# Retention and a low-rank mixer on one core: every engine's order planned by a list scheduler inside the kernel, persistent buffers, and the first u^T built in PSUM from x

## The chip, the cores and the metric

The kernel runs on one core of a Trainium2 chip. A core has a matrix engine (TensorE, "PE" in the profile; "PEld" is its loading of weights), VectorE (DVE), ScalarE (ACT), GpSimd (POOL) and SyncE (SP), which here only issues DMA transfers. In these traces each engine works through its own instructions in the order that the program gives to it, so an instruction that waits holds up all behind it. PE's results go to PSUM, which both kernels divide into eight banks of 128 x 512 float32, and the other engines copy them from there to SBUF.

The metric is device time in microseconds (us), lower is better. The kernel before takes 380.89 us (median of three runs, 378.45 to 381.08).

## The reference, cut to what matters

```python
# batch 8, heads 8, seq 576, head_dim 64  ->  d_model 512, d_ff 2048, rank 32
scores = scale * q @ k^T
ret    = scores * Dmat[h]          # Dmat = gamma_h^(i-j) for i >= j, else 0
x      = (ret @ v)                 # laid out as (batch, seq, heads*head_dim)
u      = x + V^T @ (U^T @ x)       # mixes along the sequence, rank 32
out    = u + relu(u @ w_ch1) @ w_ch2
```

Both kernels factor the decay into a scale on v and one on the result, keep a running state k^T v per chunk of 128 rows, and work on bf16 tiles with float32 sums. Two batches are 1152 rows, which are nine chunks of 128. Chunk 4, called `XC`, holds the last 64 rows of one batch and the first 64 of the next. Counted in batches there are eight groups of work; each consists of a "front" (load q, k and v, transpose q and k, scores, retention, x, U^T x, u, transpose u) and an MLP (two large matrix products, Y1 with w_ch1 and Y2 with w_ch2). The even groups' MLPs have four chunks, the odd ones' five.

The MLPs are most of the work. While PE does the MLP of one group, the front of the next is slipped in between. So the kernel has a start without any MLP (the first front), a stretch in which the weights are still being loaded, and then a steady state.

## The kernel before

Every front is a list of items with an estimated cost, and so is every MLP. A small function merges the two lists by cost shares, and what it emits is the order of PE, POOL and SP. The order on VectorE and ScalarE is left to the framework.

```python
def interleave(main, fill, lead=0.0, end=1.0):
    tm = sum(c for c, _ in main) or 1
    tf = sum(c for c, _ in fill) or 1
    i = j = 0
    dm = df = 0.0
    while i < len(main) or j < len(fill):
        if j >= len(fill) or (
            i < len(main) and dm / tm <= lead + (end - lead) * df / tf
        ):
            dm += main[i][0]
            main[i][1]()
            i += 1
        else:
            df += fill[j][0]
            fill[j][1]()
            j += 1
# [...] the pools, the constants, the items themselves
        def T(c):                                    # transpose q and k of a chunk
            # [...]
            if not pe_transpose:
                nc.sync.dma_start_transpose(
                    out=qkT, in_=t[:, 0:2, :, :].rearrange("p j h d -> p (j h d)")
                )
                return
            # [...] eight transposes on PE, one copy on ACT
# [...]
    with tc.manual_schedule(engines={PE, POOL, SPQ}):
        early_consts()
        for c in A_CH:
            load_chunk(0, c)                         # k, q, v of a chunk, float32, on SP
            if c == 1:
                load_mixer()
            if c == 3:
                load_w1([0])                         # weights: DMAs that cast, on POOL's queue
        interleave([], front_items(0, [], True, 0))  # only this front transposes on PE
        load_w1(range(1, dff // W1B))
        load_w2()
        for a in chunks_of(1):
            load_chunk(*a)
        for g in range(2 * NP):
            main = mlp_items(g // 2, g % 2, sts[g // 2])
            fill = front_items(g + 1, chunks_of(g + 2)) if g + 1 < 2 * NP else []
            interleave(main, fill, 0.35 if g == 0 else 0.05, 0.9)
```

`lead` and `end` say over which part of the MLP's time the front is spread. Line numbers such as L426 in the profile are lines of this file: L214 the DMA transpose of q and k, L237 the running state, L254 the scores, L281 their mask on VectorE, L294 retention times v, L361 U^T x, L366 its copy by ACT (`a_sb`), L376 and L379 the way back (V), L390 the DMA transpose of u, L426 Y1 and L437 Y2.

## Time and profile before

| | before |
|---|---|
| median of three runs | 380.89 us |
| span of the profiled run | 381.3 us |
| PE busy | 329.2 us, 86% |
| DVE, ACT, POOL busy | 37%, 32%, 16% |
| first matmul of the first MLP | 41.8 us |
| first matmul of the second MLP; its u^T complete | 93.0; 95.6 us |
| last matmul ends | 377.3 us |

The page of the profile first. The first line gives busy time, share of the span and instructions of each engine. The rows `PE`, `PEclk` and `DMA` cut the span into 40 slices of 9.5 us and give the busy share, the granted TensorE clock and the DMA engines' busy share in tenths (9 is 90% or more). The last line shown gives shares of the chain that ended last, followed back from the last instruction.

```profile
...
PE 329.2 (86%) x2440; PEld 176.1 (46%) x2440; DVE 142.9 (37%) x199; ACT 123.2 (32%) x244; POOL 62.4 (16%) x86
...
PE   2655794887997999999998989998999999999995
...
PEclk9999996799899999999999999999999999999999
DMA  9999999995995149995994279997991480040012
...
PE 56%; DMA 18%; SPq 13%; DVE 6%; issue 3%; ACT 2%; POOL 1%; DVEq 0%; POOLq 0%
...
```

PE is full nearly everywhere from slice 11 on; the first ten slices are poor, and there the DMA engines are at 9. Only 56% of the chain is PE. Slices 7 and 8 also show a clock of 0.6 and 0.7. The same by stretch, from the windows view (us of the window, then busy time with the number of instructions of each engine, the clock, DMA share and GB/s; the DMA share counts overlapping packets and is not used here):

```profile
...
0.00:41.80 41.80, 20.61 (x194) 13.14 (x195) 20.32 (x41) 11.96 (x17) 22.62 (x44) 1.00 1.22 194
41.80:95.60 53.80, 42.08 (x255) 18.57 (x255) 17.53 (x23) 12.87 (x22) 14.63 (x16) 0.90 1.10 184
95.60:343.00 247.40, 232.23 (x1788) 124.49 (x1788) 101.62 (x130) 84.78 (x174) 25.16 (x27) 0.99 0.80 142
343.00:381.30 38.30, 34.27 (x204) 19.90 (x204) 3.46 (x5) 13.56 (x31) 0.00 (x0) 1.00 0.11 42
...
```

In the second window PE is busy for 42.08 of 53.80 us, in the third for 232.23 of 247.40: 11.7 and 15.2 us without any matmul. The fourth, the last MLP alone, has nothing in it that could be gained. (In the first stretch PE has little to do at all.) What PE waits for is in the view of waits (engine, tile and line, what ended the wait, us in total, number of times, the longest):

```profile
...
PE po L294 <- DVE ret L281: 9.6, 10, 2.6
...
PE psc L254 <- DMA qkT<-qkv: 5.7, 2, 4.6
...
PE ph L376 <- ACT a_sb L366: 2.7, 4, 0.7
PE ps_y_936 L426 <- DMA uT<-ut: 1.9, 1, 1.9
PE ps_y_2800 L426 <- DMA uT<-ut: 1.6, 1, 1.6
...
```

These are short waits: for the masked scores, for a DMA transpose of q and k, for `a_sb`, and for the transposes of u by DMA with which every MLP starts. The longest one after the start lies in the second stretch. PE's timeline (start, us, the matmuls, and in brackets the idle time before them with what ended it):

```profile
...
56.30 1.03 PE L426 MATMUL ps_y_622<-uT,w_sb 128*128 128x512 bf16 x4
61.98 0.60 PE L254 MATMUL psc<-qkT 64*128 64x128 bf16 x8 [4.65 <-DMA qkT<-qkv]
...
62.73 1.89 PE L426 MATMUL ps_y_648<-uT,w_sb 128*128 128x512 bf16 x4
...
```

PE stands still for 4.65 us and then runs the same four matmuls at 1.89 us that took 1.03 before. It waits for a transpose that the DMA queue of SP issued late; in SP's timeline two transposes hold the queue for 14 us:

```profile
...
46.74 14.01 SPq L214 DMA_TRANSPOSE qkT<-qkv  x2
...
```

### The profile page before, as it was taken

To read this page: it belongs to the slowest core of one execution; us is meant where nothing else is said; L and a number is where in the kernel's file an instruction comes from. 1 tells how busy PE (TensorE), PEld (TensorE's weight loads), DVE (VectorE), ACT (ScalarE), POOL (GpSimd) and SP (SyncE) were. 2 spreads that over 40 slices of the span, in tenths; PEclk is the share of its full clock that TensorE was granted. 3 is DMA by queue.
4 is the path that set the end of the run, shared out by engine and by line. 5 is a ranking of instruction groups with operands and counts; after the bars stand their busy time and mean duration, and the time that the engine had idled before them with its cause. 6 is when DMAs were issued, how large, how long until landed. Compare 5 with 4: busy or idle time off the path is not lost.

```text
span 381.3 us, 5987 instructions
## 1 busy us (share of the span) xinstructions
PE 329.2 (86%) x2440; PEld 176.1 (46%) x2440; DVE 142.9 (37%) x199; ACT 123.2 (32%) x244; POOL 62.4 (16%) x86
## 2 busy tenths in 40 slices
PE   2655794887997999999998989998999999999995
PEld 1432341433673444544664435444764445447642
DVE  4454201555252342544335324552544424340021
ACT  3322361200572006501771035303660056007600
POOL 2746821221022000121021001220121000000000
PEclk9999996799899999999999999999999999999999
DMA  9999999995995149995994279997991480040012
GB/s 181 206 210 179 199 196 186 206 185 132 191 212 97 57 110 194 202 211 136 175 228 83 73 126 218 186 173 157 218 196 40 114 153 2 28 125 29 0 57 83
DMA packets 173659, 54.81 MB, mean 144 GB/s; under 512 B 164864, under 2 KB 169024, under 8 KB 173632
## 3 DMA queue, kind: packets, MB, share of 16 engines
q1 hardware_dynamic: 167840, 50.09, 73.6%
q0 software_dynamic: 5792, 4.34, 7.5%
q8 instruction: 19, 0.31, 0.4%
q14 instruction: 8, 0.07, 0.1%
HBM read 37.00 MB, written 9.44 MB: 122 GB/s over the span
## 4 chain that ended last, share of the span: by engine, by line
PE 56%; DMA 18%; SPq 13%; DVE 6%; issue 3%; ACT 2%; POOL 1%; DVEq 0%; POOLq 0%
DMA stage_t<-in_q_dram 8%; SPq L190 7%; DMA uT<-ut 4%; SPq L214 4%; DMA stage_t<-in_v_dram 3%; DVE ret L281 3%; PE po L294 2%; PE psc L254 2%; PE psa L361 2%; PE ph L379 1%; SPq L390 1%; DVE o_sb L443 1%; DVE qkv L194 1%; DMA qkT<-qkv 1%; DMA U_A<-in_moe_U_dram 1%
## 5 line engine op out<-in xcount | busy, mean ns | idle before, releaser
L426 PEld LDWEIGHTS <-w_sb 128*128 128x128 bf16 x768 | 72.2, 100 | 55.9 <-issue 17.3
L195 POOL TENSOR_TENSOR qkv<-stage_t,vscale 128x512 bf16<-128x512 f32 x36 | 38.1, 1060 | 216.2 <-DMA stage_t<-in_v_dram 156.0
L281 DVE TENSOR_TENSOR ret<-psc,tri 128x1024 bf16<-128x1024 f32 x32 | 39.1, 1223 | 50.9 <-PE psc L254 50.9
L194 DVE CAST qkv<-stage_t 128x1024 bf16<-128x1024 f32 x36 | 25.8, 718 | 64.4 <-DMA stage_t<-in_q_dram 64.4
L300 DVE TENSOR_TENSOR xt<-po,qscale 128x512 bf16<-128x512 f32 x36 | 24.8, 689 | 17.6 <-PE po L294 17.5
L366 ACT ACTIVATE a_sb<-psa 128x512 bf16<-128x512 f32 x8 | 4.8, 597 | 80.5 <-PE psa L361 76.5
L385 DVE TENSOR_TENSOR ut<-ph,xt 128x512 bf16<-128x512 f32 x36 | 24.6, 689 | 14.5 <-PE ph L379 14.4
L294 PE MATMUL po<-qkv,ret 128*128 128x64 bf16 x288 | 15.6, 201 | 9.6 <-DVE ret L281 9.6
L254 PE MATMUL psc<-qkT 64*128 64x128 bf16 x288 | 16.0, 238 | 8.8 <-DMA qkT<-qkv 5.7
L294 PEld LDWEIGHTS <-ret 128*128 128x128 bf16 x288 | 13.5, 103 | 19.6 <-DVE ret L281 15.1
L244 ACT ACTIVATE s_sb<-pss 128x512 bf16<-128x512 f32 x32 | 19.0, 593 | 5.4 <-PE pss L237 5.4
L254 PEld LDWEIGHTS <-qkT 64*128 64x128 bf16 x288 | 9.1, 102 | 22.3 <-issue 10.1
L237 PEld LDWEIGHTS <-qkv 128*128 128x128 bf16 x128 | 10.5, 105 | 6.9 <-issue 1.9
L237 PE MATMUL pss<-qkv 128*128 128x128 bf16 x112 | 12.0, 235 | 1.8 <-ACT s_sb L244 1.0
L437 PEld LDWEIGHTS <-y_3686 128*128 128x128 bf16 x80 | 7.8, 98 | 9.3
L437 PEld LDWEIGHTS <-y_929 128*128 128x128 bf16 x80 | 7.8, 101 | 9.3 <-issue 1.1
L437 PEld LDWEIGHTS <-y_1861 128*128 128x128 bf16 x80 | 7.6, 98 | 8.6
L437 PEld LDWEIGHTS <-y_2793 128*128 128x128 bf16 x80 | 7.6, 98 | 8.6
L221 PE MATMUL pst<-ident,qkv 128*128 128x128 bf16 x40 | 5.2, 311 | 7.3 <-DVE qkv L194 7.3
L226 ACT ACTIVATE qkT<-pst 128x1024 bf16<-128x1024 bf16 x5 | 5.1, 1024 | 15.1 <-PE pst L221 15.1
L163 POOL DMA_DIRECT2D w_sb<-in_moe_w_ch_dram x16 | 9.3, 597 | 3.5 <-DMA w_sb<-in_moe_w_ch_dram 3.5
L437 PEld LDWEIGHTS <-y_1457 128*128 128x128 bf16 x64 | 6.1, 98 | 7.1
(522 smaller groups left out, 536.7 us busy)
## 6 DMA issues: line engine op xcount, KB each, us to landing
out_dram<-o_sb SPq DMA_DIRECT2D x36, 256.0 KB, 2.2
stage_t<-in_k_dram SPq DMA_DIRECT2D x32, 256.0 KB, 3.9
stage_t<-in_q_dram SPq DMA_DIRECT2D x32, 256.0 KB, 5.1
stage_t<-in_v_dram SPq DMA_DIRECT2D x32, 256.0 KB, 5.1
w_sb<-in_moe_w_ch_dram POOLq DMA_DIRECT2D x16, 128.0 KB, 7.2
w_sb<-in_moe_w_ch_dram POOLq DMA_DIRECT2D x8, 256.0 KB, 11.5
stage_t<-in_k_dram SPq DMA_DIRECT2D x8, 128.0 KB, 4.8
stage_t<-in_q_dram SPq DMA_DIRECT2D x8, 128.0 KB, 4.8
```

The costliest lines, as they stand in the source:

```text
L190: nc.sync.dma_start(out=f[rows, j, :, :], in_=dram[b, :, t0:t0 + L, :].rearrange("h s d -> s h d"),)
L194: nc.vector.tensor_copy(out=t[:, 0:2, :, :], in_=f[:, 0:2, :, :])
L195: nc.gpsimd.tensor_tensor(out=t[:, 2, :, :], in0=f[:, 2, :, :], in1=vscale[:, c, :, None].to_broadcast([P, H, D]), op=ALU.mult,)
L237: nc.tensor.matmul(pss[:, hp, :], t[:, 1, 2 * hp:2 * hp + 2, :].rearrange("p h d -> p (h d)"), vt[:, 2 * hp:2 * hp + 2, :].rearrange("p h ...
L244: nc.scalar.activation(out=s_sb, in_=pss, func=AF.Copy)
L254: nc.tensor.matmul(psc[:, hl, hp, :], qkT[pb:pb + HALF, NHP + hp, :], qkT[pb:pb + HALF, hp, :], start=True, stop=True,)
L281: nc.vector.tensor_tensor(out=ret.rearrange("p (hp hl) i -> p hl hp i", hl=2), in0=psc, in1=mask[:, None, None, :].to_broadcast([P, 2, NHP ...
L294: nc.tensor.matmul(po[:, hl, hp * D:(hp + 1) * D], ret[:, h, :], t[:, 2, h, :], start=(c == 0 and hp == 0), stop=True, skip_group_check=True,)
L300: nc.vector.tensor_tensor(out=xt.rearrange("p (hp hl d) -> p hl hp d", hl=2, d=D), in0=po[:, :, 0:NHP * D].rearrange("p hl (hp d) -> p hl ...
L385: nc.vector.tensor_tensor(out=ut, in0=ph, in1=st["x", c], op=ALU.add)
L426: nc.tensor.matmul(ps[:, 0:n], w1_sb[:, cc, f * P:(f + 1) * P], uT[:, cc, t0:t0 + n], start=(cc == 0), stop=(cc == NCC - 1),)
L437: nc.tensor.matmul(ps, st["y1"][:, f, i * P:(i + 1) * P], w2_sb[:, f, :], start=(f == 0), stop=(f == NF - 1),)
```

## The change

The merging function goes. The kernel now describes each piece of work as an `Op` with a duration on its engine, dependencies, a priority and the buffers that it takes and gives back, and simulates all five engines and the DMA rings at build time. Of the operations that could start earliest, the one with the best priority is emitted next. The outcome fixes the order of all engines. Four further changes come with it: the buffers are persistent slots; the second group's fronts transpose on PE (no DMA transposes while the weights load); the first u^T is built directly in PSUM, as x^T (16 PE transposes) plus four matmuls that add V^T (U^T x), with U padded by zeros to 128 columns; and the weights come by plain float32 DMAs on SP and are cast by POOL or VectorE. Y1 of the odd groups goes from two halves of 320 columns to 512 + 128, and the stores go from SP to POOL's queue. The diff, cut to its core:

```diff
-def interleave(main, fill, lead=0.0, end=1.0):
-    [...]
+class Plan:
+    LAT = {"PE": 230.0, "ACT": 80.0, "DVE": 80.0, "POOL": 90.0}
+    DMA_LAT = 1700.0
+    DMA_AHEAD = 4500.0
+    [...]
+    def run(self):
+        [...]
+        def add(o):
+            o.ready = max([d.vis for d in o.deps], default=0.0)
+            for e, dur in o.engs:
+                avail[e].append((o, dur))
+        [...]
+                t, o, dur = min((c for c in cand if c[0] <= te + 1e-6), key=lambda c: c[1].prio)
+                k = (te, o.prio)
+                if best is None or k < best[0]:
+                    best = (k, e, o, dur, te)
+            [...]
+            if e == "SP":
+                ring = max(ring, t + 700.0) + o.work
+                o.vis = ring + self.DMA_LAT
 [...]
+    def load(p, c, which="AB", prio=0.0, first=True, early=False):
+        [...]
+        for o, (j, dram) in enumerate(((1, k), (0, q), (2, v))):
+            [...]
+            got[j] = DMA(470.0 * L / P + 60 * (n - 1), 1180.0 * L / P, fn, prio=prio + 0.01 * o,
+                         acq=[("stage", key)] if o == 0 else (), deps=[got[1]] if o else ())
 [...]
+    def ST(p, c, prio, half=None):                 # running state, in the bank ps_s
+        [...]
+        o = pl.op("PE", 230.0 + (190 if half else 0), fn,
+                  [st["v", c, w], st["k", c, w], None if first else prev], prio,
+                  acq=[("pss", ("S", p, c if first else 0))] if first else ())
 [...]
+        def xT(c, cc):                             # first u^T: x^T into PSUM ...
+            def fn(e):
+                mm(acc(cc)[:, c * P:(c + 1) * P], xs[slot("x", (0, c))][:, cc * P:(cc + 1) * P],
+                   ident, start=(c == 0), stop=True)
+            return fn
+        [...]                                      # ... plus (U^T x)^T V on top of it
+                mm(acc(cc), a_sb[0][:, cc * P:(cc + 1) * P], VV[:, 0:4 * P], start=False, stop=True)
 [...]
+    start_batch()
+    load_w(-800.0)
+    [...]
+    mlp(0, fixed(10.0, 10.0 + W, NU(0)))
+    front(1, dict(at=lambda n: -100.0 + n, load=500.0, cast=1, tr=2), pe=True)
+    for g in range(1, NG):
+        [...]
+            lo, hi = (0.02, 0.88)
+        [...]
-    with tc.manual_schedule(engines={PE, POOL, SPQ}):
-        [...]
+    with tc.manual_schedule():
+        for o, e in pl.run():
+            o.fn(e)
```

In `load`, q and v depend on `got[1]`, the DMA of k, and in the planner an operation becomes ready at its dependencies' `vis`, which for a DMA is its landing. And in `ST`, the first chunk of a running state takes the PSUM bank `pss` whenever it is free; the U^T x of the group before takes the same bank.

## The prediction

> **What bounds the kernel now.** PE is busy 86% of 381 us (the page). Counting all matmul columns at full rate (2.4 per ns: four 512-column matmuls per 0.86 us), PE needs 302.5 us, so 78 us are lost. PE's timeline shows three stretches:
>
> 1. 0 to 41.8 us (first MLP matmul, L426): about 10 us of PE work. Five q/k/v chunks are loaded; then the first u^T is built serially: psa at 32.4, four rounds of ph, DVE add, PE transpose, ACT copy, 1.8 us each.
> 2. 41.8 to 95.6 us (second group's MLP): about 40 us of work in 54. L426 takes 1.71 us per four until 46.8 and again from 62 to 70, where the slices show clock 0.6 and 0.7. The Trainium skill ("TensorE: Matmul & The Clock Gate", Part 1) says that a sparsely used array runs at half rate; this trace agrees (1.71 against 0.86 us). PE stands 4.65 us for a DMA transpose; the DMA queue's timeline shows two transposes holding SP for 14 us.
> 3. 95.6 to 381: 286 us for about 258 us of columns. From 95 to 343 the matmuls' starts exceed their columns' time by 22.8 us: some 4 are a fixed 2.5 ns each, 3 a halved clock, 10 the switches around 64-row matmuls, the rest waits for uT, a_sb and scores. The last group (343 to 377) loses nothing; 3.5 us of add and store follow.
>
> **What the change does.** Columns rise to 306.3 us (more transposes on PE). HBM bytes stay 37 MB. Weights move from casting DMAs on POOL's queue to plain DMAs on SP with 16 casts on POOL and DVE (a DVE cast of 128x1024 took 0.72 us; on POOL I estimate 1.2 to 2). The casting packets had 25.8 us of 16 engines; I estimate the same for plain ones, so the DMA floor for two groups and the weights stays at 60 us. The gain is order. In the instruction order, w1 blocks stand before the first group's last q, so its MLP hardly starts earlier: 36 to 41 us. But the second group uses no DMA transposes, and the first u^T needs only U^T x, four matmuls and four evictions.
>
> **Sum (estimates).** Stretch 1: -3. Stretch 2: second MLP at 83 instead of 95.6, a further -9. Stretch 3: uT, a_sb and score waits hidden by the order, -8; less halved clock, -3. Slips of a fixed plan against real DMA times, and POOL issuing 34 stores between scalings of v: +3. Total -20, and up to -6 more if the plan holds well: **355 us, 8 times in 10 between 342 and 369**. Chances: faster by over 2% 0.93, within 2% 0.05, slower 0.02.
>
> **What would show it.** Right: first MLP matmul near 38 us, second group's near 83; no PE wait over 2 us after 50; no clock of 0.6 in the slices; excess over columns from there to the last group under 15 us; no 14 us of transposes on SP. Wrong: PE waiting for POOL (late casts, w2 above all), DMA share well below 1 in the first 60 us because SP is blocked on buffers, or new waits for transposes where a planned DMA comes late.
>
> **What would make it wrong.** With fixed orders on all engines, one late DMA stalls all behind it; POOL casts may be much slower than planned. Conversely, if plain weight loads beat the casting ones, stretch 2 shrinks more and the time nears 342.

## The result

| | before | after |
|---|---|---|
| median of four runs | 380.72 us | 356.68 us |
| lowest to highest | 378.45 to 381.08 | 354.47 to 358.27 |
| ratio, 95% interval | | 0.9366 (0.9317 to 0.9415) |

The ratio is the mean time of one kernel's runs over that of the other's of the same rounds, so it is not quite the ratio of the medians. The result is right. Executions over 1.5% slower than the fastest of the same kernel are left out of the means. The kernel is 24.0 us faster by the medians. The profiled run of the changed kernel happens to be its fastest, so the spans of the two profiles (381.3 and 352.6) differ by 28.7 us, a little more than the kernels do; what follows splits those 28.7.

The page of the profile after, the same lines:

```profile
...
PE 319.7 (91%) x2520; PEld 167.2 (47%) x2520; DVE 156.1 (44%) x215; ACT 128.2 (36%) x214; POOL 63.7 (18%) x88
...
PE   0464699999999979998999999999999999999994
...
PEclk9995999999999999999999999999999999999998
DMA  8999999999999999999999948954213300150012
...
PE 80%; DMA 12%; SPq 3%; DVE 2%; issue 1%; ACT 1%; POOL 0%; DVEq 0%; ACTq 0%
...
```

PE's busy share rises to 91%, from the sixth slice on it is full, and 80% of the chain that ended last is PE. The clock of 0.6 in slices 7 and 8 is gone, but a 5 stands in the fourth slice. By stretch, cut at the same events as before:

```profile
...
0.00:44.20 44.20, 19.47 (x227) 13.56 (x227) 22.51 (x45) 17.28 (x27) 10.63 (x22) 0.88 1.05 222
44.20:82.10 37.90, 37.47 (x304) 18.92 (x298) 23.59 (x34) 17.38 (x29) 9.85 (x10) 1.00 1.05 260
82.10:310.00 227.90, 224.97 (x1779) 115.83 (x1777) 104.73 (x131) 81.61 (x139) 40.55 (x52) 1.00 0.76 156
310.00:352.60 42.60, 37.80 (x223) 18.91 (x221) 5.27 (x8) 11.94 (x20) 2.70 (x5) 0.97 0.17 53
...
```

In the second window PE now lacks 0.4 us, and in the third 2.9 of 227.9. Counted from event to event (starts of the first and second MLP, last matmul, end):

| stretch | before | after | difference |
|---|---|---|---|
| 1: start to first MLP | 41.8 | 44.2 | +2.4 |
| 2: first to second MLP | 51.3 | 37.9 | -13.4 |
| 3: second MLP to last matmul | 284.3 | 265.7 | -18.6 |
| tail | 3.9 | 4.8 | +0.9 |

So stretch 1, for which a part of the change was written, became longer, and the gain comes from the other two.

Not all of it is waiting. PE also works at half clock, and the clock row hides most of that: the trace's clock record begins with the first change, and what comes before counts as full. PE's timeline of the kernel before shows what the clock was. Groups of four matmuls of Y1 start 1.71 us apart in the opening (43.41, 45.12, 46.83), where the row says 9, and 0.86 to 0.87 apart after the first record, at 47.1 (47.82, 48.69, 49.55):

```profile
...
43.41 1.91 PE L426 MATMUL ps_y_532<-uT,w_sb 128*128 128x512 bf16 x4
...
47.82 1.03 PE L426 MATMUL ps_y_550<-uT,w_sb 128*128 128x512 bf16 x4
...
```

In all 14 traces the matmuls of a burst are spaced at half rate up to the first record (but for the first pair of a burst, which is closer). The record stands at 22.3 us after and between 20.4 and 60.5 in the other runs. From the traces follows an estimate of what this is worth. For every matmul that starts at half clock, take its columns at the half-rate spacing of this trace less those at the full-rate spacing: the sum is 19.5 us before (9.5, 6.7 and 3.3 in the three stretches) and 6.1 after (all in the first). PE's idle time up to the last matmul falls from 48.1 to 28.1 us. So of the 28.7 us, 20.0 are idle time and 13.4 are half clock; 3.8 of more matmul columns and 0.9 of tail go the other way. In stretch 2 alone 9.5 are idle time and 6.7 half clock. This is bookkeeping, not an experiment: PE idles and runs at half clock in the same places, and a faster clock in front of a late load may only have made PE wait longer there.

The waits of PE after, as above:

```profile
...
PE ps_big_t L334 <- DVE qkv_t L280: 12.5, 3, 5.6
...
PE ps_s L237 <- DVE qkv_t L287: 3.8, 4, 1.9
PE ps_big_t L237 <- DMA uT_t<-u_t: 2.0, 2, 1.8
PE ps_o L237 <- DVE ret_t L418: 1.9, 2, 1.6
...
```

All waits of the first two lines lie before 45 us, but for one of 0.3 at 50.5. After that, the longest is 1.8 us, once, for a transpose of u. The start of the kernel shows where stretch 1 went. PE's timeline:

```profile
...
30.64 0.61 PE L334 MATMUL ps_big_t<-ident,qkv_t 128*128 128x128 bf16 x4 [5.63 <-DVE qkv_t L280]
...
40.60 0.38 PE L237 MATMUL ps_s<-qkv_t 64*128 64x128 bf16 x4 [1.95 <-DVE qkv_t L287]
...
44.24 1.04 PE L237 MATMUL ps_big_t<-uT_t,w_sb 128*128 128x512 bf16 x4
...
```

PE stands 5.63 us until VectorE has cast a q. The chain that ended last names the DMA that was late, issued at 20.93 and landed 9.21 us later:

```profile
...
20.93 9.21 DMA stage_t<-in_q_dram
...
```

It is the last q of the first group. On SP's queue it stands behind three 512 KB weight blocks issued at 16.94 and two k of the second group, because the planner lets q wait for the landing of its k and uses the gap for the weights. Then, at 40.60, PE waits 1.95 us for the v of a second-group chunk, with the four matmuls that complete the first u^T standing behind it in PE's order. The first MLP could have started without either.

### The profile page after: what moved, and what is told of

Its sections match the earlier page's. It is cut to its first block, busy times and chain, and to the rows that moved or that the text cites. A ratio compares the mean times of both kernels' runs of the same rounds, so it can differ in the third digit from the quotient of the medians.

```text
span 352.6 us, 6119 instructions
## 1 busy us (share of the span) xinstructions
PE 319.7 (91%) x2520; PEld 167.2 (47%) x2520; DVE 156.1 (44%) x215; ACT 128.2 (36%) x214; POOL 63.7 (18%) x88
## 4 chain that ended last, share of the span: by engine, by line
PE 80%; DMA 12%; SPq 3%; DVE 2%; issue 1%; ACT 1%; POOL 0%; DVEq 0%; ACTq 0%
PE ps_big_t L237 67%; PE ps_s L237 5%; DMA stage_t<-in_q_dram 4%; PE ps_o L237 4%; DMA stage_t<-in_v_dram 4%; PE ps_sc L237 3%; DMA wst_t<-in_moe_w_ch_dram 2%; DMA uT_t<-u_t 2%; SPq L266 1%; DVE o_sb L666 1%; PE ps_big_t L334 1%; SPq L787 0%; DVE qkv_t L287 0%; DVE ret_t L418 0%; ACT s_sb L375 0%
## 5 line engine op out<-in xcount | busy, mean ns | idle before, releaser
L237 PE MATMUL ps_big_t<-uT_t,w_sb 128*128 128x512 bf16 (+1 forms) x768 | 134.5, 326 | 2.0 <-DMA uT_t<-u_t 2.0
L237 PE MATMUL ps_big_t<-w_sb,y_t 128*128 128x512 bf16 x576 | 133.9, 379 | 0.0
L618 ACT ACTIVATE y_t<-ps_big_t 128x512 bf16<-128x512 f32 x128 | 76.1, 597 | 63.0 <-PE ps_big_t L237 63.0
L237 PEld LDWEIGHTS <-y_t 128*128 128x128 bf16 x576 | 54.9, 98 | 63.5
L666 DVE TENSOR_TENSOR o_sb<-ps_big_t,u_t 128x512 f32<-128x512 f32 x36 | 24.9, 690 | 69.6 <-PE ps_big_t L237 69.3
L287 POOL TENSOR_TENSOR qkv_t<-stage_t,vscale 128x512 bf16<-128x512 f32 x30 | 31.5, 1051 | 98.3 <-DMA stage_t<-in_v_dram 56.1
L481 DVE TENSOR_TENSOR x_t<-ps_o,qscale 128x512 bf16<-128x512 f32 (+1 forms) x37 | 25.5, 690 | 51.1 <-PE ps_o L237 51.1
L418 DVE TENSOR_TENSOR ret_t<-ps_sc,tri 128x1024 bf16<-128x1024 f32 (+1 forms) x34 | 40.4, 1189 | 14.3 <-PE ps_sc L237 14.3
L672 POOL DMA_DIRECT2D out_dram<-o_sb x34 | 19.6, 576 | 138.8 <-DVE o_sb L666 134.8
L280 DVE CAST qkv_t<-stage_t 128x1024 bf16<-128x1024 f32 (+2 forms) x37 | 27.7, 749 | 25.1 <-DMA stage_t<-in_q_dram 24.7
L334 PE MATMUL ps_big_t<-ident,qkv_t 128*128 128x128 bf16 (+1 forms) x80 | 7.9, 250 | 17.4 <-DVE qkv_t L280 12.5
L237 PEld LDWEIGHTS <-qkT_t 64*128 64x128 bf16 (+1 forms) x552 | 14.7, 99 | 11.3 <-issue 6.8
L558 DVE TENSOR_TENSOR u_t<-ps_s,x_t 128x512 bf16<-128x512 f32 x20 | 13.7, 687 | 12.6 <-PE ps_s L237 12.5
```

The source lines that it names most:

```text
L237: nc.tensor.matmul(*a, skip_group_check=True, **kw)
L280: nc.vector.tensor_copy(**args)
L287: eng.tensor_tensor(out=t[rows, 2, :, :], in0=f[rows, 2, :, :], in1=vscale[rows, c, :, None].to_broadcast([L, H, D]), op=ALU.mult,)
L334: nc.tensor.transpose(pst[:, j * NHP + hp, rows], t[rows, j, 2 * hp:2 * hp + 2, :].rearrange("p h d -> p (h d)"), ident[rows, rows],)
L418: nc.vector.tensor_tensor(out=ret[slot(*rk)].rearrange("p (hp hl) i -> p hl hp i", hl=2)[rows, :, :, rows], in0=ps_sc[rows, :, :, rows], i ...
L481: nc.vector.tensor_tensor(out=xs[slot(*xk)].rearrange("p (hp hl d) -> p hl hp d", hl=2, d=D)[rows], in0=ps_o[rows, :, 0:NHP * D].rearrange ...
```

## The experiments

Twelve kernels ran, each beside the kernel before on the same chip. "Stretches" are those of the table above, from the profiled run. All results agree with the reference. One run of b_end80 (390.73) and two of a_wcast were slow; the medians include them, the ratios do not. Medians of different batches of runs differ by a microsecond or two for the kernel before (380.12, 382.31, 380.38 and 379.68), so the ratios are the better measure.

| kernel | median | ratio to before (95%) | stretches 1 / 2 / 3 | half clock: opening + recorded |
|---|---|---|---|---|
| before | 380.72 | 1 | 41.8 / 51.3 / 284.3 | 47.1 + 17.1 us |
| after | 356.68 | 0.937 (0.932 to 0.942) | 44.2 / 37.9 / 265.7 | 22.3 + 10.2 us |
| a_earlyq | 415.94 | 1.092 (1.083 to 1.100) | 36.8 / 64.2 / 306.7 | 21.0 + 78.5 us |
| a_noxt | 370.67 | 0.973 (0.967 to 0.979) | 67.7 / 33.4 / 263.7 | 22.7 + 44.4 us |
| a_dmat | 367.53 | 0.966 (0.959 to 0.974) | 46.8 / 47.9 / 266.6 | 22.0 + 27.3 us |
| a_auto | 357.67 | 0.939 (0.933 to 0.945) | 46.6 / 38.6 / 268.0 | 46.8 + 3.4 us |
| b_pe1 | 380.81 | 0.996 (0.992 to 1.000) | 42.2 / 52.4 / 280.2 | 44.7 + 6.8 us |
| b_end80 | 386.33 | 1.007 (1.000 to 1.014) | 42.2 / 48.8 / 286.0 | 47.0 + 13.7 us |
| b_manual | 417.73 | 1.093 (1.087 to 1.098) | 52.1 / 55.1 / 303.6 | 57.4 + 30.7 us |
| a_wcast | 357.99 | 0.929 (0.923 to 0.935) | 49.9 / 41.3 / 263.5 (slow run) | 44.4 us |
| a_earlyq_ps | 364.17 | 0.953 (0.947 to 0.960) | 37.9 / 55.7 / 265.6 | 20.4 + 20.5 us |
| a_y320sp | 362.28 | 0.950 (0.944 to 0.956) | 47.2 / 38.1 / 270.6 | 47.0 + 6.8 us |
| best1 | 348.70 | 0.915 (0.910 to 0.920) | see below | 28.3 us |
| best1_noxt | 356.48 | 0.938 (0.933 to 0.943) | 55.8 / 35.0 / 261.1 | 60.5 us |

The half-clock column gives first the opening, from the start to the first clock record, which the spacing of the matmuls shows to be at half rate, and then the sum of the later stretches in which the record shows 0.5 and that start before the last matmul.

### a_earlyq: let q and v of the first group be issued behind k's issue, not behind its landing

```diff
 [...]  # `soft`, a new field of Op, empty by default
         def add(o):
-            o.ready = max([d.vis for d in o.deps], default=0.0)
+            o.ready = max([d.end if d in o.soft else d.vis for d in o.deps], default=0.0)
 [...]
+            if early and p == 0 and c <= XC and which != "B" and o:
+                got[j].soft = (got[1],)
```

> The changed kernel, but the q and v loads of the first group are issued right behind k instead of after k has landed in the plan. In the changed kernel's trace PE waits 5.63 us for the last q of the first group (issued at 20.93, landed 30.14 behind three weight blocks) and reaches the first MLP matmul at 44.2 us. Theory (after that matmul PE never lacks work, so each us of an earlier start is a us of time): first MLP matmul at 35 to 39 us, no half clock at 25 to 35, time 5 to 8 us lower. Rival (the DMA floor of about 60 us for two groups and the weights binds): the start is earlier but PE waits later, between 45 and 80 us, for weights or second-group chunks, and the time moves by less than 2 us.

Measured: 415.94 us, slower than before by 9%. Both theories fell, though the first half of one held: the first MLP starts at 36.8, 7.4 us earlier. Everything after that is worse. One changed readiness gave a different plan for the whole kernel. PE's timeline of this run:

```profile
...
69.66 0.38 PE L238 MATMUL ps_s<-qkv_t 128*128 128x128 bf16 x4 [2.47 <-POOL qkv_t L290]
71.92 0.38 PE L238 MATMUL ps_s<-qkv_t 128*128 128x128 bf16 x4 [1.88 <-POOL qkv_t L290]
...
90.79 2.29 PE L238 MATMUL ps_s<-x_t,UU 128*128 128x512 bf16 x5 [0.74 <-ACT s_sb L378]
...
```

At 69.66 and 71.92 PE waits for POOL's scaling of a v. These matmuls are the running state of the third group, and they have taken the bank `ps_s` before the second group's U^T x, which needs the same bank. That U^T x comes only at 90.79, and the second MLP starts at 101.0. The lag is handed on from group to group: a front that comes late is then done in one piece with no MLP work in between, PE waits for each short step (in this run's view of waits 16.1 us in 16 waits for masked scores), and the sparse use shows in the clock, which falls to half again and again:

```profile
...
PEclk9986999866999969995699988997799977999999
...
```

The simulation inside the kernel says so too: the planned end that the kernel's own code computes at build time is 397 us for this kernel and 342 for the changed one. It is no measured time and lies 19 and 15 us below the medians, but it ranks them rightly.

### a_earlyq_ps: the same, and the running state may take the bank only after the previous group's U^T x

One dependency is added to a_earlyq:

```diff
-                  [st["v", c, w], st["k", c, w], None if first else prev], prio,
+                  [st["v", c, w], st["k", c, w], (ld.get("MA") if p or half else None) if first else prev], prio,
 [...]
         o = MA(p, par, t(nn + 0.9), bank)
+        ld["MA"] = o
```

> a_earlyq (early q and v loads, 416 us) with one more dependency in the plan: the running state of group g may take the PSUM tile ps_s only after the U^T x of group g-1 has used it. Theory (a_earlyq lost its time because the third group's running state took ps_s at 70 us and the second group's U^T x, due at 78, stood until 91, and this lag was handed on from group to group): 358 to 368 us, PE idle after the second MLP's start back below 6 us instead of 24.9, the second MLP at 84 to 92. Rival (the time went because the PE array lacked work at the start and its clock fell; the order is not the cause): 400 us or more, half-clock stretches after 100 us as in a_earlyq.

Measured: 364.17 us. This theory held in its time (its second MLP, at 84 to 92, was missed by 1.6 us): 52 us come back by one dependency, so who takes the shared bank first is what made a_earlyq slow. Stretch 1 is 37.9 and stretch 3 as good as after's (265.6 against 265.7). Stretch 2 is still 17.8 us longer than after's: its second MLP starts at 93.6. The early start of the first MLP brought nothing in this plan: between the two MLPs PE waits 7.3 us for casts of w2 blocks that landed late (four waits on L818, the longest 3.4), and half clock is recorded for 10.2 us.

### a_noxt: the first u^T as in the other groups, through u and a transpose of u

```diff
-        banks = [("big", "ucc0"), ("big", "ucc1"), ("sc", "ucc"), None]
-        [...]  # x^T and V^T (U^T x) into PSUM, four copies to uT
-            MH(0, 0, c, 20.0 + c, c)
+            MH(0, 0, c, base + 61 + c, c)
+            MT(0, 0, c, base + 61 + c, pe=True, first=c == 0)
```

> The changed kernel with one part undone: the first u^T is built as before (ph, DVE add, four PE transposes and an ACT copy per chunk) instead of in PSUM. Theory (the part shortens the serial tail before the first MLP matmul): first MLP matmul 3 to 5 us later than 44.2, time 3 to 5 us higher. Rival (the second group's data bounds that stretch anyway): the time rises by less than 1 us, PE standing less between 45 and 80.

Measured: 370.67 us, 14 us slower than the changed kernel, with a first MLP at 67.7: neither the 3 to 5 us of the theory nor the less than 1 of its rival. Not all of this is the cost of the older path. The planner also put a transpose of a second-group chunk in front of the last pieces of the first u^T, and its q had not been cast:

```profile
...
59.65 0.61 PE L334 MATMUL ps_big_t<-ident,qkv_t 128*128 128x128 bf16 x4 [7.01 <-DVE qkv_t L280]
```

The clock had fallen to half long before this wait, at 26.1, and stayed there without a break for 44.4 us (fourth to eighth slice):

```profile
...
PEclk9995555699999999999999999999999999999999
...
```

The stretch 2 that follows is shorter than after's (33.4 against 37.9), since the second group's work has been done in the meantime. So this run shows that the part and the plan cannot be judged apart: it gives 14 us as the worth of the part under this plan. The run best1_noxt, below, gives another figure under a better one.

### a_dmat: the second group transposes by DMA again

```diff
-            if pe:
+            if pe and c == XC:
                 t_pe(p, c, w, t(n) - 1.0, first=w != "B")
 [...]
-            MT(p, par, c, t(nn + 1.2 + 0.15 * i), pe=pe, first=i == 0)
+            MT(p, par, c, t(nn + 1.2 + 0.15 * i), pe=False, first=i == 0)
```

> The changed kernel with one part undone: chunks 5 to 8 and the u of the second group are transposed by DMA again. Theory (in the loading phase a DMA transpose waits behind loads and holds the SP queue): PE waits of several us between 45 and 85, the second group's MLP 4 to 10 us later than 82.1, the time up by as much. Rival (the scheduler hides it, and 2 us of PE work are saved): within 1.5 us of the changed kernel, or faster.

Measured: 367.53 us, 10.9 more than after. The second MLP starts at 94.7 instead of 82.1, 12.5 later. So the theory held in place, and its size was a little over the range of 4 to 10. The waits are not of several us, but short and many, from 86.9 on at half clock, while PE has nothing else to do:

```profile
...
80.79 0.41 PE L237 MATMUL ps_o<-qkv_t,ret_t 128*128 128x64 bf16 x8 [1.47 <-DVE ret_t L418]
...
87.42 0.61 PE L237 MATMUL ps_s<-qkv_t 128*128 128x128 bf16 x4 [1.21 <-DVE u_t L558]
...
94.67 1.87 PE L237 MATMUL ps_big_t<-uT_t,w_sb 128*128 128x512 bf16 x4 [1.92 <-DMA uT_t<-u_t]
```

### b_pe1: the kernel before, with PE transposes for the second group alone

```diff
-            fill = front_items(g + 1, chunks_of(g + 2)) if g + 1 < 2 * NP else []
+            fill = front_items(g + 1, chunks_of(g + 2), pe_t=g == 0) if g + 1 < 2 * NP else []
 [...]  # and a flag by which the mixer still computes U^T x
```

> The kernel before with one part of the change alone: the second group's q, k and u are transposed on PE, not by DMA. Theory (the DMA transposes in the loading phase cost the 14 us on SP and PE's 4.65 us wait and its half clock): the second group's MLP starts 5 to 10 us earlier than 95.6, time 5 to 10 us lower. Rival (the loads themselves are late, so PE waits for the casts instead): less than 2 us.

Measured: 380.81 us against 382.31, a ratio of 0.996 whose interval just reaches 1. The same part that is worth 11 us under the plan is worth next to nothing in the old order. The wait for the DMA transpose is gone, and another one has taken its place, in the same microseconds, for VectorE's masked scores:

```profile
...
65.15 0.61 PE L294 MATMUL po<-qkv,ret 128*128 128x64 bf16 x8 [6.34 <-DVE ret L281]
...
```

VectorE's trace shows where this wait comes from: the mask, at 63.88, stands behind a cast that began at 63.27 after waiting 3.83 us for a q to land. So in this place the rival is what is seen: the load is late, whatever transposes it. PE's idle time in stretches 1 and 2 together is 34.6 us here (23.0 + 11.6) and 31.1 (21.2 + 9.9) in the kernel before.

### b_end80: the kernel before, with every later front done by 80% of the MLP's time

```diff
-            interleave(main, fill, 0.35 if g == 0 else 0.05, 0.9)
+            interleave(main, fill, 0.35 if g == 0 else 0.05, 0.9 if g == 0 else 0.8)
```

> The kernel before with its fill finished at 80% instead of 90% of each MLP. Theory (part of stretch 3's loss is plain order: uT arrives about 1 us late at six group starts, because the mixer stands too near the end): the waits for uT at the group starts vanish (about 6 us), time 3 to 6 us lower. Rival (the waits move into the fill, which then runs ahead of its loads): waits for scores or q loads grow by as much, time within 2 us.

Measured: 386.33 us, ratio 1.007 (1.000 to 1.014), which is no clear loss. Finishing the front earlier should take away the waits for u^T with which each MLP starts. But a front that is drawn together meets its own loads and its own short steps:

```profile
...
PE po L273 <- POOL qTx L267: 10.2, 3, 4.1
PE psc L254 <- DMA qkT<-qkv: 7.7, 7, 3.3
...
```

In the kernel before, the same two lines were 0.9 us in one wait and 5.7 us in two. The waits moved.

### b_manual: the kernel before, with VectorE's and ScalarE's order fixed as well, as emitted

```diff
-    with tc.manual_schedule(engines={PE, POOL, SPQ}):
+    with tc.manual_schedule():
```

> The kernel before with all engines, DVE and ACT too, in the order in which the program emits them. Theory (an order alone, without a plan behind it, helps nothing: casts that wait for loads would then stand in front of masks): slower, by 2 to 20 us. Rival (the framework's own order of DVE and ACT was the loss, 8 us of PE waits for masked scores): faster by 3 us or more.

Measured: 417.73 us, 9% slower; the direction was expected, the size (+35) was not. PE's waits for the masked scores went from 9.6 to

```profile
...
PE po L294 <- DVE ret L281: 39.4, 12, 14.4
...
```

and the longest from 2.6 to 14.4. Here the copies and casts stand on VectorE in the order in which the merging function calls the items, and a cast of a late q blocks the mask behind it (at 70.79 a cast begins after 17.33 us of waiting for its q, and the mask follows at 71.40). So a fixed order on all engines is no gain in itself. The changed kernel fixes the same engines, but by a plan that reckons with when the data come.

### a_auto: the changed kernel, with VectorE's and ScalarE's order left to the framework

```diff
-    with tc.manual_schedule():
+    with tc.manual_schedule(engines={ET.PE, ET.Pool, ET.SP}):
```

> The changed kernel, but only PE, POOL and SP keep the planned order; DVE and ACT are ordered by the framework, as in the kernel before. Theory (what counts is the order on PE and the DMA queue): within 2 us. Rival (a planned order on all engines is what removed the waits for scores and masks): PE waits after 82 us return to 8 us or more, time up by 5 us or more.

Measured: 357.67 us, ratio 0.939 against 0.937. The theory held: what the plan gives lies in the order of PE, POOL and SP.

### a_wcast: the changed kernel, with the weights by casting DMAs on POOL's queue again

```diff
 [...]  # the planner also counts these DMAs on its rings
-                    nc.sync.dma_start(
-                        out=wst[slot(*key)].rearrange("p (c n) -> p c n", n=512),
-                        [...]
-                ld["w1", fb].append(pl.op("POOL", 1150.0, cast, [o], prio + 5 + fb, rel=[key],
-                                          alt=[("DVE", 700.0)]))
+                    nc.gpsimd.dma_start(
+                        out=w1_sb[:, 2 * hc:2 * hc + 2, fb * 512:(fb + 1) * 512],
+                        [...]
+                ld["w1", fb].append(pl.op("POOL", 900.0, fn, [cons], prio + fb + hc * 0.1, work=1500.0))
```

> The changed kernel with one part undone: the weights come by casting DMAs of POOL's queue, 16 of them, straight into bf16, without staging and casts. Theory (packets cost the same either way, 25.8 against 25 us of 16 engines, so it is their place in the queue that counts): loads of the first group slow down where casting DMAs run beside them, first MLP matmul 0 to 4 us later, time 0 to 4 us higher. Rival (plain 2 KB loads are what let the second stretch shrink): MLP of the second group over 5 us later, time up by over 5.

Measured: 357.99 us over four runs, of which two (360.36, the profiled one, and 363.96) were slow; the two fast ones are 355.62 and 354.92, and the ratio of 0.929 is theirs. The difference from the changed kernel is within its scatter, so the way of the weights is not a source of the gain, nor a clear loss. The profile is of a slow run, so only its order of events is used: the first MLP starts later, at 49.9, with long waits at the start, among them one for a scaled v,

```profile
...
PE ps_s L239 <- DVE qkv_t L289: 7.2, 2, 6.8
...
```

and stretch 3 makes up for it. The Trainium skill ("DMA: Bandwidth & Descriptors", section "Issuing engines are not separate DMA queues") says that transfers from different engines end up on the same 16 DMA engines, and that issuing from several only saves issue time. These two kernels agree: 355.3 (the mean of the two fast runs) with the weights on POOL's queue, 356.68 with them on SP's.

### a_y320sp: the changed kernel, with the old halves of 320 columns and the stores on SP

```diff
-            last = Y1(f)
-            if par and f % 4 == 3:
-                last = Y1b(f - 3)
+            if par:
+                Y1h(f, 0)          # 320 columns
+                last = Y1h(f, 1)   # 320 columns
+            else:
+                last = Y1(f)
 [...]
-                pl.op("POOL", 900.0, store, [a], o.prio, rel=[ok], work=700.0)
+                DMA(400.0, 700.0, store, deps=[a], prio=o.prio, rel=[ok])
```

> The changed kernel with two of its steady-state parts undone at once: the odd groups' first product in two blocks of 320 columns as before (instead of one of 512 and a batched one of 4 x 128), and all stores issued by SP instead of POOL. Theory (stretch 3 was won by the planned order on PE alone): PE idle after the second MLP's start stays below 6 us, time within 4 us of the changed kernel. Rival (the block shape or the queue of the stores made the difference): PE idle there back to 10 us or more, time up by 8 us or more.

Measured: 362.28 us, 5.6 more than after, between what the two theories said. Stretch 3 is 270.6 long: of the 18.6 us that it gained, 13.7 (284.3 less 270.6) remain with the old shape and the old store queue. A part of the 4.9 that are lost are waits for transposes of u, whose DMAs now share SP's queue with the stores:

```profile
...
PE ps_big_t L237 <- DMA uT_t<-u_t: 3.7, 3, 1.7
...
```

That line was 2.0 us with two waits in the changed kernel. Half clock, recorded for 6.8 us of its stretch 3 and not at all in that of the changed kernel, may be another. Which of the two edits costs what was not tried.

### best1: the changed kernel with truer DMA times in its plan, the early q, and earlier fronts

```diff
-    DMA_LAT = 1700.0
+    DMA_LAT = 2200.0
 [...]  # `soft` in Op and in add, as in a_earlyq
-            got[j] = DMA(470.0 * L / P + 60 * (n - 1), 1180.0 * L / P, fn, prio=prio + 0.01 * o,
+            got[j] = DMA(470.0 * L / P + 60 * (n - 1), 1340.0 * L / P, fn, prio=prio + 0.01 * o,
+            if early and o:
+                got[j].soft = (got[1],)
 [...]
+            if g == 0 and f0 == 0:
+                deps += ld["w2", 2]
 [...]
-                o = DMA(450.0, 1500.0, fn, ...)          # both kinds of weights
+                o = DMA(450.0, 1600.0, fn, ...)
 [...]
-    load_w(-800.0)
+    load_w(-590.0)
 [...]
-    front(1, dict(at=lambda n: -100.0 + n, load=500.0, cast=1, tr=2), pe=True)
+    front(1, dict(at=lambda n: -100.0 + 8.0 * n, load=500.0, cast=1, tr=2), pe=True)
 [...]
-            lo, hi = (0.02, 0.88)
+            lo, hi = (0.0, 0.8)
 [...]
-            front(g + 1, dict(at=at, load=45.0, cast=20.0, tr=16.0))
+            front(g + 1, dict(at=at, load=55.0, cast=20.0, tr=24.0))
```

The first Y2 of the first group also waits for a later weight block, so that its accumulators do not sit in PSUM banks while the weights are still on their way.

> A candidate to beat the changed kernel. The planner's DMA costs are set to what its trace shows (256 KB of q, k or v 1.34 us instead of 1.18, 512 KB of weights 1.6 instead of 1.5, 2.2 us of latency instead of 1.7); q and v of the first two groups are issued right behind k; the second group's loads alternate with the weights instead of following them; Y2 of the first group takes no PSUM bank before its third w2 block is there; the fronts stand somewhat earlier in their MLP (lo 0.0, hi 0.8, load 55, tr 24). Theory (the start was bound by the order of the loads, and the plan was wrong there because its DMA was too fast): first MLP matmul at 36 to 40 us, no PE wait over 3 us after it, 349 to 353 us. Rival (the DMA floor of some 60 us binds): PE waits between 45 and 80 for second-group data, 356 us or more.

Measured: 348.70 us (347.84 to 349.70, six runs), ratio 0.915 (0.910 to 0.920). It beats both kernels: 8.0 us below the changed one and 32 below the one before by the medians. Its page:

```profile
...
PE 318.5 (92%) x2477; PEld 167.2 (48%) x2520; DVE 156.3 (45%) x216; ACT 128.7 (37%) x214; POOL 62.0 (18%) x87
...
PE   2568897999999999999999999999999999999995
...
PEclk9999999999999999999999999999999999999999
...
PE 84%; DMA 5%; DVE 4%; ACT 2%; SPq 2%; issue 1%; POOL 1%; ACTq 0%
...
```

The first MLP starts at 35.0, a little earlier than expected, and the clock is at full rate from 28.3 on. The second group's Y1 is mixed into the first MLP, and from 35.0 to the last matmul at 342.0 PE lacks only 8.4 us at most (some matmul records are missing, and count as idle). Here the MLPs overlap, so the three stretches of the table do not apply.

### best1_noxt: best1 with the first u^T by the older path

The edit to a_noxt, applied to best1.

> best1 (348.7 us) with the first u^T built as before (ph, add, PE transposes, copies) instead of in PSUM: the same part undone as in a_noxt, but under a plan whose loads are timed as the chip times them. Theory (in a_noxt a third at most of the 14 us was the part itself; the rest was a new order that put a transpose of the second group, whose q was not there for 7 us, in front of the first MLP, and 44 us of half clock after it): 351 to 356 us, no half-clock stretch over 11 us. Rival (the part itself is worth 14 us: the serial tail starves PE): 360 us or more, with a long half-clock stretch.

Measured: 356.48 us, 7.8 over best1. The rival's number was not reached, and the theory's range was missed by half a microsecond. But its other sign, no half-clock stretch over 11 us, failed: the first clock record stands at 60.5 here and at 28.3 in best1, and up to there the matmuls are spaced at half rate. PE's idle time up to the last matmul is the same in both profiles, 23 us, while half clock costs 17.4 us here and 6.7 in best1 by the estimate used above. So what the part is worth under this plan appears as a longer opening at half clock; what it would be worth without that is not shown. Under a plan that fits better, building u^T in PSUM is worth about 8 us, not the 14 of a_noxt; the first MLP starts at 55.8 here, 20.8 later than in best1, and more than half of that is made up, because PE does second-group work in the meantime and lacks only 0.1 us from there to the last matmul.

## Why the prediction was right or wrong, point by point

**The time and the direction: right.** 356.68 was measured, 355 predicted, and the ratio's whole interval lies well below 0.98. That the sum came so close is partly luck: stretch 1 was 5.4 us worse than forecast, and stretches 2 and 3 were 4.4 and 7.6 better.

**Stretch 1, "36 to 41 us ... -3": wrong.** It was 44.2, and +2.4 in the table. The reading of the order was right as far as it went ("w1 blocks stand before the first group's last q"), but I took it to cancel the gain, not to exceed it. That q took 9.21 us to land and PE stood 5.63 us for it. And I looked only at the load order, not at what else PE had to do in between: second-group work stood in front of the last four matmuls of u^T (1.95 us). a_earlyq and a_earlyq_ps, where only the first cause is removed (the rest of the plan shifts with it), start the first MLP at 36.8 and 37.9, so it cost some 6 to 7 us.

**"The first u^T needs only U^T x, four matmuls and four evictions": the step is right, its worth in time was hidden.** From the first transposes after the last q to the first MLP it took 13.6 us after (30.64 to 44.24) and 14.9 before (26.89 to 41.76), since the second group's pieces fill the gaps. Taking the part out costs 14.0 us in one plan and 7.8 in another.

**"No clock of 0.6 in the slices": wrong as written.** The old ones went, but slice 4 shows 5, a stretch of 10.2 us from 25.7 on. It begins after a window of 3.41 us in which PE was busy for 0.34 of it. Did it cost time? That is not shown. The profiled run, with a mean clock of 0.982, is the fastest (354.47), and the other three, with 0.997 to 0.999, took 356.36 to 358.27. But the mean counts all before the first record as full: a_auto, with 0.995, ran at half clock for its first 46.8 us. So the other three may have had more half clock than the profiled run, and not less. The slices also hide the half clock of the kernel before up to 47.1 us; the prediction saw the part of it from 41.8 on (1.71 us per four).

**Stretch 2, "second MLP at 83": right.** It starts at 82.1. The term was under-sized all the same, because the first MLP started later: the stretch became 13.4 us shorter where I had -9. The reason given (no DMA transposes in the second group) is shown by a_dmat: +10.9 us, with a second MLP at 94.7. By the bookkeeping above, 9.5 us less of idle time and 6.7 less of half clock went into the 13.4, against 2.8 of added columns. b_pe1 adds what the prediction did not say: without the plan the same part gains nothing.

**Stretch 3, "-8 ... -3": right in kind, under-sized.** It is 18.6 us shorter. PE's idle time in the third window fell from 15.2 to 2.9 us, by 12.3. Between 95.6 and 343 us the trace before shows 15 gaps of over 0.25 us without a matmul, which sum to 14.7 us: 5.4 for transposes of u (six), 4.9 for masked scores (three), 2.1 for `a_sb` (three), and 2.3 for three others. After, from 82.1 to 310, there are two, of 1.8 and 0.75. Half clock was recorded for 6.8 us in stretch 3 before and not at all after, which is worth at most 3.4 us.

**"10 the switches around 64-row matmuls": wrong.** I had counted starts of matmuls in excess of their columns and put what was left over down to switching between shapes. But where nothing is waited for, a block of eight score matmuls takes 0.23 us and the eight 64-row matmuls behind it 0.21 in the trace before (starts at 234.75 and 234.98, the next Y1 at 235.19), and 0.24 and 0.21 after (93.91, 94.15 and 94.36). The same instructions are left, and the same spacing, and yet the loss is gone. It was waits. Had I summed the gaps instead, I would have put the waits at 14.7 us and not at 8, and the reason would have been right.

**"Slips of a fixed plan ... +3": right in kind, in a place not named.** PE's waits for POOL sum to 0.2 us after. The stores on POOL delay nothing that can be seen. The slip is in stretch 1, by loads that the plan thought would land sooner. The plan inside the kernel has its first three MLPs at 39.2, 76.3 and 119.0; measured were 44.2, 82.1 and 126.7. With the DMA costs of best1 alone put into it, the same code plans 44.3, 81.6 and 126.7. That is an agreement of a model with one trace, not a proof, but it is why those costs went into best1.

**POOL's cast, "1.2 to 2": too high.** It is 1.04 us, as this groups view shows (busy, mean ns). The planner has 1150 ns for it, close enough to matter little.

```profile
...
L287 POOL TENSOR_TENSOR qkv_t<-stage_t,vscale 128x512 bf16<-128x512 f32 x30 | 31.5, 1051 | 98.3 <-DMA stage_t<-in_v_dram 56.1 <-PE ps_o L237 27.4 <-issue 10.0
...
L796 POOL CAST w_sb<-wst_t 128x1024 bf16<-128x1024 f32 x5 | 5.2, 1038 | 16.4 <-DMA wst_t<-in_moe_w_ch_dram 16.4
...
```

**"If plain weight loads beat the casting ones": they did not.** a_wcast is the same within scatter.

**What stays open.** The rest of a_noxt's 14 us is not split between the longer path, the misplaced transpose and 44.4 us at half clock (the plan inside the kernel, which knows of no half clock, already ends 14.6 later than that of the changed kernel: 356.7 against 342.1). No run held the clock up by extra matmuls, so what half clock costs, in a_earlyq (78.5 us after the opening) as in the openings of all kernels, is not separated from the idle time that comes with it. The persistent slots, with slightly other numbers of buffers, were never undone, so what they give is not separated from the order. And best1 changes several things at once; the early q with the corrected costs and the earlier fronts were not run apart.

The result in one sentence: about half of the gain (11 of 24 us, a_dmat) needs the second group's transposes on PE, most of the rest is won in the steady state by the planned order together with the persistent slots (13.7 us of it remain in a_y320sp), neither is had in the old order (b_pe1, b_end80, b_manual), and the planned start gave some 2 us back, with weights loaded ahead of the last q.

## What to carry to other kernels

When waits are short and many, taking one away in an order that is not planned only moves it: b_pe1 and b_end80 removed the wait that they were aimed at and gained nothing, while one plan for the order of PE and the DMA queue removed them together. A plan is as good as its DMA times and its rules on shared buffers: compare its planned starts with a trace, correct the costs of the transfers, and say by a dependency who takes a shared PSUM bank first, because one free choice there cost 52 us. The share of the 28.7 us that went with half clock, some 13, shows only in the spacing of the matmuls, so compare that with the clock row before trusting the row. To find what a kernel loses, sum the gaps of the busiest engine by what ended them, rather than subtract an ideal rate and name the remainder.

## What the Trainium skill lacked or had wrong

- "TensorE: Matmul & The Clock Gate", Part 1, section "What's actually happening": it gives a half clock or a full one and a window of 3413 ns, and the traces agree (0.5, and stretches of 3.4, 6.8, 10.2, 13.7, 17.1 and 44.4 us, all multiples of it). Its table names an idle window as what lowers the clock, and the section "A second HAM failure mode: psum-queue depth-cycling" adds frequent short idle times without a number. Here, over all traces, it fell after windows in which PE was busy for anything from 0.0 to 0.5 of the time, and in a_earlyq, at 147.3 us, after one with 0.62.
- The same place calls the ramp under 1% of a typical span. Here the opening at half clock lasts from 20.4 us (a_earlyq_ps) to 60.5 us (best1_noxt), 28.3 of 346.1 even in best1, where PE is busy for at most 0.68 of each window before the last of them; and later half clock held for 78.5 of 411.7 us (a_earlyq) and 44.4 of 368.6 (a_noxt). The section "HAM oscillation — how this bites in real kernels" describes that case for a loop of loads; what it costs in a start that waits for loads anyway is not shown here either.
- No page that I read says that the clock record of a trace begins with the first change and leaves out the opening: 47.1 us at half rate before, by the spacing of the matmuls, without a record.
- The same page, section "Back-to-back issue gap": the isolated gap of N/2.4 + 2.5 ns is what a stream of matmuls does here, 0.86 us for four of 512 columns, so 216 ns each. Its sustained figure of 131 ns for 512 columns was seen nowhere.
- "Perfetto Trace Analysis", section "Matmuls", advises independent groups of matmuls to rotate through PSUM banks. No page that I read says what happens where one bank serves several stages of neighbouring groups and the order of its owners is left free: 52 us between a_earlyq and a_earlyq_ps.
- I found no measured figure for a float32 to bf16 cast of 128 x 1024 on GpSimd beside VectorE: 1.04 us here, against 0.69 on VectorE.
